# Attention by 128-token tile over all heads, transposes in bf16, woven by hand into an FFN of 512-token chunks

## The chip, the cores and the metric

One core of a Trainium2 chip runs the whole program; the other cores of the chip are idle. The metric is device time in microseconds (us): the median of repeated executions. TensorE is PE in the profile (PEld its weight loads), VectorE is DVE, ScalarE ACT, GpSimd POOL, and SyncE SP, which here only issues DMAs.

## The reference

Attention with a short window, then a maxout FFN. Each query sees the 8 first keys and the 96 last ones up to itself, with a bias that falls linearly with distance (ALiBi); softmax without anything unusual. The shapes are batch 4, 8 heads, 768 tokens, 64 columns a head; the FFN takes 3,072 rows of 512 through three weights of 512 x 768, keeps the largest of the three products, and multiplies by 768 x 512. All inputs and outputs are fp32.

```python
scores = scale * np.matmul(q, k.transpose(0, 1, 3, 2))
keep = is_global | is_local          # first 8 keys, or 0 <= distance < 96
scores = np.where(keep, scores + bias, -1e9)
a = softmax(scores)
x = np.matmul(a, v)                  # to rows of batch*seq, 8 heads x 64
h = np.maximum(np.maximum(x @ w1, x @ w2), x @ w3)
out = h @ w_out
```

## The kernel before, in words

The attention is tiled by batch and by pair of heads (lines 119 and 120): 16 pairs, each over all 768 tokens, that is six tiles of 128. Q, K and V of a pair come in by six DMAs (143 to 145) on two queues, SP for q and k, ACT for v. POOL casts v (149) and makes a second copy vg (150, 151) whose first 8 rows are the first 8 tokens, so that the block on the left of the diagonal can serve the global keys too. PE transposes twelve tiles of q and k in fp32 (161) into PSUM; ACT and DVE bring them to bf16 in SBUF as qT and kT (164 to 170). Scores (186, 196) are computed with keys on the partitions; ACT takes exp of them (203), and DVE multiplies by wmask, which holds the exponential of the bias and zero outside the window (209, 213). Then PE multiplies with v and a column of ones (235), DVE takes the reciprocal of the sums (242) and normalises (243), PE transposes the result in bf16 (249), and DVE writes it into xT (251), which holds all 3,072 tokens.

The FFN runs over six chunks of 512 tokens (256). For each of six blocks of 128 hidden columns PE computes three products of four matmuls each (263) into three PSUM banks, ACT copies the first out (269), DVE takes the maximum with the second and third (270, 271) into ht. Four output tiles of 128 tokens then take six matmuls each (275) into a PSUM tile, ACT copies it out (278), SP stores it (279). The weights come in while the third pair is set up (121 to 134).

Nothing in this text fixes the order of an engine's work: the code is written pair by pair and then chunk by chunk, and the framework's scheduler orders each engine's queue, so that FFN work of a batch whose four pairs are done mixes with the attention of the next batch. A chunk needs all heads of its tokens, so the first can begin when batch 0 is through, and the last batch has chunks of earlier tokens beside it as long as the scheduler has any left. PSUM has eight banks: three rotate in psA (tp, sp, xtp and po), two in psU, three in psH.

Of the kernel before, what the change touches and what calls it, by code (L numbers as in the profile page):

```python
# [19 lines left out]
def kernel(  # L21
# [13 lines left out]
    nc = tc.nc  # L35
# [6 lines left out]
    NHP = H // 2  # L42
    DM = H * D
    DFF = moe_w1.shape[1]
    NTOK = B * S
# [4 lines left out]
    for qc in range(1, NT):  # L50
        blocks.append((qc - 1, qc, True))
        blocks.append((qc, qc, False))
    NBLK = len(blocks)

    def dpos(qc):
        return 2 * qc

    def spos(qc):
        return 2 * qc - 1

    SGRP = [list(range(0, 4)), list(range(4, 8)), list(range(8, 11))]
    WKIND = [0 if (not b[2] and b[1] == 0) else (1 if not b[2] else 2)
             for b in blocks]

    persist = ctx.enter_context(tc.tile_pool(name="persist", bufs=1))
    wpool = ctx.enter_context(tc.tile_pool(name="wpool", bufs=1))
    qkv_pool = ctx.enter_context(tc.tile_pool(name="qkv", bufs=4))
    vv_pool = ctx.enter_context(tc.tile_pool(name="vv", bufs=3))
    qkT_pool = ctx.enter_context(tc.tile_pool(name="qkT", bufs=3))
# [26 lines left out]
    nc.vector.tensor_copy(rbase[:, 2, :], rbase[:, 2, :].bitcast(mybir.dt.int32))
    nc.gpsimd.affine_select(rbase[:, 2, :], rbase[:, 2, :], base=(NL - 1) - 128,
                            pattern=[[-1, 128]], channel_multiplier=1,
                            compare_op=ALU.is_ge, fill=BIGD)
    nc.vector.memset(rbase[0:NG, 2, :], float(NL))  # L100
    nc.vector.tensor_copy(rbase[:, 0, :], rbase[:, 1, :])
    nc.vector.tensor_scalar_min(rbase[0:NG, 0, :], rbase[0:NG, 0, :], float(NL))
    wmask = persist.tile([128, H, 3, 128], BF16, name="wmask")
    for h in range(H):
        nc.scalar.activation(wmask[:, h, :, :], rbase, AF.Exp,
                             bias=0.0, scale=-slopes[h])
# [11 lines left out]
    if True:  # L118
        for b in range(B):
            for jp in range(NHP):  # L120
# [196 lines left out]
```

## Time and profile before

| | |
|---|---|
| median of 3 runs | 285.93 us (285.15 to 286.02) |
| span of the profiled execution | 283.5 us |
| that execution's own time | not listed; the median is 2.4 us over its span |
| PE busy, matmuls | 237.2 us, 1,536 |
| DVE busy | 137.9 us |
| ACT busy | 102.4 us |
| POOL busy | 34.7 us |
| mean granted clock of PE | 0.916 |
| read from HBM, written | 25.17 MB, 6.29 MB |

A row of a view gives an engine, the line of the code, what it writes and reads, how often, and then busy time and mean. PEclk is the granted clock of TensorE: 1.00 is 2.4 GHz and 0.50 is 1.2 GHz. The chain of waits runs from the last instruction back to what released it, and is printed in order of time. Ends of matmuls are modelled, so a busy PE need not be at its peak.

### The profile page before, as it was taken

To read this page: it belongs to the slowest core of one execution; us is meant where nothing else is said; L and a number is where in the kernel's file an instruction comes from. 1 tells how busy PE (TensorE), PEld (TensorE's weight loads), DVE (VectorE), ACT (ScalarE), POOL (GpSimd) and SP (SyncE) were. 2 spreads that over 40 slices of the span, in tenths; PEclk is the share of its full clock that TensorE was granted. 3 is DMA by queue.
4 is the path that set the end of the run, shared out by engine and by line. 5 is a ranking of instruction groups with operands and counts; after the bars stand their busy time and mean duration, and the time that the engine had idled before them with its cause. 6 is when DMAs were issued, how large, how long until landed. Compare 5 with 4: busy or idle time off the path is not lost.

```text
span 283.5 us, 4068 instructions
## 1 busy us (share of the span) xinstructions
PE 237.2 (84%) x1536; PEld 126.2 (45%) x1536; DVE 137.9 (49%) x286; ACT 102.4 (36%) x198; POOL 34.7 (12%) x60
## 2 busy tenths in 40 slices
PE   0406668788999978999999788769999999999994
PEld 0303426446456446455455545534444444444441
DVE  1227654535759545658657554560251550551540
ACT  0435141452462452453554353242514214214222
POOL 2530202202112112012112200000000000000000
PEclk9999999775999995999999676676999999999999
DMA  8999999996373483370550000001513004003003
GB/s 167 218 333 355 310 269 225 216 186 147 79 168 74 97 168 84 85 166 5 111 112 2 0 2 0 0 2 54 205 39 141 7 0 150 0 0 149 2 0 149
DMA packets 81332, 31.73 MB, mean 112 GB/s; under 512 B 75936, under 2 KB 75936, under 8 KB 81312
## 3 DMA queue, kind: packets, MB, share of 16 engines
q1 hardware_dynamic: 56224, 25.17, 34.5%
q10 hardware_dynamic: 25088, 6.29, 11.5%
q8 instruction: 12, 0.20, 0.3%
q14 instruction: 8, 0.07, 0.1%
HBM read 25.17 MB, written 6.29 MB: 111 GB/s over the span
## 4 chain that ended last, share of the span: by engine, by line
PE 69%; DMA 12%; DVE 10%; ACT 6%; issue 2%; ACTq 0%; SPq 0%
PE h L263 33%; PE po L275 12%; PE tp L161 9%; DMA wst<-in_moe_w_dram 6%; PE sp L186 6%; ACT pt L203 5%; PE ut L235 4%; DVE pt L213 4%; DMA vraw<-in_v_dram 4%; PE xtp L249 3%; PE sp L196 3%; DVE xpair L243 3%; DMA wst<-in_moe_w_out_dram 2%; DVE rz L242 1%; DVE w L128 1%
## 5 line engine op out<-in xcount | busy, mean ns | idle before, releaser
L263 PE MATMUL h<-xT,w 128*128 128x512 bf16 x432 | 105.8, 387 | 0.4 <-ACT h L269 0.2
L263 PEld LDWEIGHTS <-w 128*128 128x128 bf16 x432 | 41.1, 99 | 43.6 <-issue 2.7
L203 ACT ACTIVATE pt<-sp 128x512 bf16<-128x512 f32 (+1 forms) x96 | 47.5, 564 | 30.5 <-PE sp L196 30.1
L270 DVE TENSOR_TENSOR h<-h,h 128x512 bf16<-128x512 bf16 x36 | 24.6, 682 | 40.6 <-PE h L263 39.8
L186 PE MATMUL sp<-qT,kT 64*128 64x256 bf16 x192 | 32.2, 294 | 13.1 <-DVE kT L168 12.2
L269 ACT CAST h<-h 128x512 bf16<-128x512 f32 x36 | 21.1, 585 | 53.6 <-PE h L263 46.7
L275 PE MATMUL po<-wo,ht 128*128 128x512 bf16 x144 | 34.1, 397 | 0.0
L235 PE MATMUL ut<-vql,pt 128*128 128x65 bf16 x224 | 22.9, 216 | 11.8 <-DVE pt L213 10.2
L271 DVE TENSOR_TENSOR ht<-h,h 128x512 bf16<-128x512 bf16 x36 | 24.6, 683 | 15.7 <-PE po L275 6.7
L213 DVE TENSOR_TENSOR pt<-pt,wmask 128x1280 bf16<-128x1280 bf16 x32 | 25.0, 821 | 13.1 <-ACT pt L203 13.1
L149 POOL CAST vql<-vraw 128x768 bf16<-128x768 f32 x16 | 13.2, 828 | 123.4 <-PE ut L235 115.5
L164 ACT ACTIVATE qT<-tp 128x512 bf16<-128x512 f32 x16 | 9.5, 596 | 49.3 <-PE tp L161 44.9
L235 PEld LDWEIGHTS <-pt 128*128 128x128 bf16 x352 | 18.0, 111 | 20.3 <-DVE pt L213 14.9
L161 PE MATMUL tp<-identf,qraw 128*128 128x128 f32 x96 | 19.2, 355 | 7.8 <-DMA qraw<-in_q_dram 7.8
L278 ACT COPY ost<-po 128x512 f32<-128x512 f32 x24 | 14.1, 587 | 30.9 <-PE po L275 30.8
L186 PEld LDWEIGHTS <-kT 64*128 64x128 bf16 x192 | 9.5, 97 | 31.4 <-DVE kT L168 21.2
L275 PEld LDWEIGHTS <-ht 128*128 128x128 bf16 x144 | 14.7, 102 | 18.3 <-issue 2.8
L196 PE MATMUL sp<-qT,kT 64*8 64x128 bf16 x128 | 19.7, 226 | 0.0
L161 PE MATMUL tp<-identf,kraw 128*128 128x128 f32 x96 | 19.5, 355 | 0.2
L249 PE MATMUL xtp<-identb,xpair 128*128 128x128 bf16 x96 | 10.9, 269 | 9.4 <-DVE xpair L243 8.8
L161 PEld LDWEIGHTS tp<-identf,qraw 128*128 128x128 f32 x96 | 15.1, 189 | 7.7 <-POOL vql L149 7.7
L243 DVE SCALAR_TENSOR_TENSOR xpair<-ut,rz 128x384 bf16<-128x384 f32 x32 | 17.7, 555 | 0.4
(35 smaller groups left out, 131.7 us busy)
## 6 DMA issues: line engine op xcount, KB each, us to landing
vraw<-in_v_dram ACTq DMA_DIRECT2D x32, 192.0 KB, 5.1
qraw<-in_q_dram SPq DMA_DIRECT2D x32, 192.0 KB, 3.8
kraw<-in_k_dram SPq DMA_DIRECT2D x32, 192.0 KB, 4.0
out_dram<-ost SPq DMA_DIRECT2D x24, 256.0 KB, 2.0
wst<-in_moe_w_dram SPq DMA_DIRECT2D x12, 384.0 KB, 6.3
wst<-in_moe_w_out_dram SPq DMA_DIRECT2D x6, 256.0 KB, 5.8
```

The lines of the kernel that those rows point to most:

```text
L161: nc.tensor.transpose(tp[:, i * 128:(i + 1) * 128], srcs[g * 4 + i], identf)
L186: nc.tensor.matmul(sps[hh][:, pos * 128:pos * 128 + w], kT[hsl, kt * 128:(kt + 1) * 128], qT[hsl, qc * 128:qc * 128 + w], start=True, stop ...
L196: nc.tensor.matmul(sps[hh][0:NG, pos * 128:(pos + 1) * 128], kT[hsl, 0:NG], qT[hsl, qc * 128:(qc + 1) * 128], start=True, stop=True)
L203: nc.scalar.activation(pts[hh][:, grp[0] * 128: grp[0] * 128 + n], sps[hh][:, 0:n], AF.Exp, bias=0.0, scale=1.0)
L213: eng.tensor_mul(pts[hh][:, 128:NBLK * 128].rearrange("p (a b c) -> p a b c", a=NT - 1, b=2), pts[hh][:, 128:NBLK * 128].rearrange("p (a b ...
L235: nc.tensor.matmul(ut[:, qc, :], pts[hh][:, bi * 128:(bi + 1) * 128], mov, start=(ci == 0), stop=(ci == len(cons) - 1), skip_group_check=True)
L243: nc.vector.scalar_tensor_tensor(out=xpair[:, :, hh, :], in0=ut[:, :, 0:64], scalar=1.0, in1=rz[:, :, None].to_broadcast([128, NT, 64]), o ...
L263: nc.tensor.matmul(ps[j], w123[dm][:, j, f * 128:(f + 1) * 128], xT[:, dm, c * CH:(c + 1) * CH], start=(dm == 0), stop=(dm == 3))
L269: nc.scalar.copy(h01, ps[0])
L270: nc.vector.tensor_max(h01, h01, ps[1])
L271: nc.vector.tensor_max(ht[:, f, :], h01, ps[2])
L275: nc.tensor.matmul(po, ht[:, f, tt * 128:(tt + 1) * 128], wo[:, f, :], start=(f == 0), stop=(f == 5))
```

## The change

The attention is no longer cut by pairs of heads but by tiles of 128 tokens, each with all eight heads, 24 tiles T in all. A tile is loaded by three DMAs, all on SP (function load). POOL casts q and k to bf16 in one instruction and v in another (cast). A tile's attention is split into units: X transposes q and k, eight 128x128 blocks in bf16, and DVE copies the result out in one instruction; POOL then makes kgT, a copy of the keys whose first 8 columns are the first 8 keys, so that window and global keys are one matmul for the left block, and vg likewise. S takes the scores of four heads into a PSUM tile of two banks, ACT takes exp of 1,024 columns at once (the scale now sits there), and DVE's mask multiply is put off until the next attention unit. A multiplies with v and normalises, for four heads. T transposes the result and writes it into xT of a 512-token chunk. FFN-1 units u_F1 have four matmuls, FFN-2 units u_F2 six.

The order of every engine's queue is now that of the program's text (manual_schedule). First come all units up to T of tile 3, the last tile of chunk 0; then each chunk's 22 FFN units are taken in turn, and after each of the first 20 one or two attention units of the next four tiles are written. The sixth chunk has none. The PSUM pools all have one buffer: S two banks, h0 to h2 one each, and one each for A, for X and T together (tag tp), and for the FFN output (po). Loads go out in a fixed list: tiles 0 to 3, w1 to w3 in nine DMAs, tile 4, w_out in three, then tiles 5 to 23 three ahead of use. The matmuls of the FFN are the same in number and shape.

```diff
--- the kernel before
+++ the kernel after
...
-    blocks = [(0, 0, False)]
...
-    xT = persist.tile([128, 4, NTOK], BF16, name="xT")
-
-    psA = ctx.enter_context(tc.tile_pool(name="psA", bufs=3, space=bass.MemoryType.PSUM))
-    psU = ctx.enter_context(tc.tile_pool(name="psU", bufs=2, space=bass.MemoryType.PSUM))
...
-        for b in range(B):
-            for jp in range(NHP):
...
-        for c in range(NCH):
...
+    CHUNK = 4
+    chunks = [list(range(c, c + CHUNK)) for c in range(0, NTT, CHUNK)]
...
+    raw_pool = ctx.enter_context(tc.tile_pool(name="raw", bufs=4))
+    cast_pool = ctx.enter_context(tc.tile_pool(name="cast", bufs=3))
+    qkT_pool = ctx.enter_context(tc.tile_pool(name="qkT", bufs=4))
+    kg_pool = ctx.enter_context(tc.tile_pool(name="kg", bufs=3))
+    p_pool = ctx.enter_context(tc.tile_pool(name="pp", bufs=5))
...
+    xb_pool = ctx.enter_context(tc.tile_pool(name="xb", bufs=3))
+    xT_pool = ctx.enter_context(tc.tile_pool(name="xT", bufs=3))
+    stage_pool = ctx.enter_context(tc.tile_pool(name="stage", bufs=12))
+    ht_pool = ctx.enter_context(tc.tile_pool(name="ht", bufs=2))
+    h01_pool = ctx.enter_context(tc.tile_pool(name="h01", bufs=3))
+    ost_pool = ctx.enter_context(tc.tile_pool(name="ost", bufs=4))
+    psS = ctx.enter_context(tc.tile_pool(name="psS", bufs=1, space=bass.MemoryType.PSUM))
+    psH = ctx.enter_context(tc.tile_pool(name="psH", bufs=1, space=bass.MemoryType.PSUM))
+    psO = ctx.enter_context(tc.tile_pool(name="psO", bufs=1, space=bass.MemoryType.PSUM))
+    psT = ctx.enter_context(tc.tile_pool(name="psT", bufs=1, space=bass.MemoryType.PSUM))
+    psP = ctx.enter_context(tc.tile_pool(name="psP", bufs=1, space=bass.MemoryType.PSUM))
...
+    def load(T):
+        b, t = divmod(T, NT)
+        r = raw_pool.tile([128, 3, H, D], FP32, name="raw", tag="raw")
+        raw[T] = r
+        sl = slice(t * 128, (t + 1) * 128)
+        for i, src in enumerate((q, k, v)):
+            nc.sync.dma_start(out=r[:, i], in_=src[b, :, sl, :].rearrange("h s d -> s h d"))
+
+    def cast(T):
+        b, t = divmod(T, NT)
+        r = raw[T]
+        qk = cast_pool.tile([128, 2, DM], BF16, name="qkb", tag="qkb")
+        qb[T] = qk
+        nc.gpsimd.tensor_copy(qk, r[:, 0:2].rearrange("p a h d -> p a (h d)"))
+        va[T] = va_first[b % 2] if t == 0 else va_ring[T % NVA]
+        nc.gpsimd.tensor_copy(va[T][:, :, 0:D], r[:, 2])
...
+    def make_vg(T):
+        b, t = divmod(T, NT)
+        if t == 0:
+            vg[T] = va[T]
+        elif t < NT - 1:
+            vg[T] = vg_ring[T % 3]
+            nc.gpsimd.tensor_copy(vg[T], va[T])
+            nc.gpsimd.tensor_copy(vg[T][0:NG], va[b * NT][0:NG])
+
+    def make_kg(T):
+        b, t = divmod(T, NT)
+        kT = qkT[T][:, 1]
+        if t == 0:
+            kgT[T] = kT
+            nc.gpsimd.tensor_copy(kg8[b % 2], kT[:, :, 0:NG])
+        elif t < NT - 1:
+            kgT[T] = kg_pool.tile([128, NP, 128], BF16, name="kgT", tag="kgT")
+            nc.gpsimd.tensor_copy(kgT[T], kT)
+            nc.gpsimd.tensor_copy(kgT[T][:, :, 0:NG], kg8[b % 2])
+
+    def u_X(T):
+        tp = psT.tile([128, 2, NP, 128], BF16, name="tp", tag="tp")
+        for a in range(2):
+            for jp in range(NP):
+                nc.tensor.transpose(tp[:, a, jp], qb[T][:, a, jp * 128:(jp + 1) * 128], identb)
+        qkT[T] = qkT_pool.tile([128, 2, NP, 128], BF16, name="qkT", tag="qkT")
+        nc.vector.tensor_copy(qkT[T], tp)
+        make_kg(T)
+        make_vg(T)
+        return []
+    def u_S(T, g):
+        b, t = divmod(T, NT)
+        sp = psS.tile([128, 2, 2, 2, 128], FP32, name="sp", tag="sp")
+        for ds in range(2 if t else 1):
+            for j2 in range(2):
+                jp = 2 * g + j2
+                for hh in range(2):
+                    hsl = slice(64 * hh, 64 * hh + 64)
+                    st = qkT[T][hsl, 1, jp] if ds == 0 else kgT[T - 1][hsl, jp]
+                    nc.tensor.matmul(sp[:, hh, j2, ds], st, qkT[T][hsl, 0, jp],
+                                     start=True, stop=True, skip_group_check=True)
+        P = p_pool.tile([128, 4, 2, 128], BF16, name="P", tag="P")
+        Pt[T, g] = P
+        spv = sp.rearrange("p a b d n -> p (a b) d n")
+        if t:
+            nc.scalar.activation(P, spv, AF.Exp, bias=0.0, scale=scale)
+            return [lambda: nc.vector.tensor_mul(P, P, wmask[:, g])]
+        nc.scalar.activation(P[:, :, 0], spv[:, :, 0], AF.Exp, bias=0.0, scale=scale)
+        return [lambda: nc.vector.tensor_mul(P[:, :, 0], P[:, :, 0], wmask0[:, g])]
...
+    def u_A(T, g):
+        b, t = divmod(T, NT)
+        op = psO.tile([128, 4, 65], FP32, name="op", tag="op")
+        P = Pt[T, g]
+        for j2 in range(2):
+            for hh in range(2):
+                h = 4 * g + 2 * j2 + hh
+                i = 2 * hh + j2
+                o = op[:, 2 * j2 + hh]
+                nc.tensor.matmul(o, P[:, i, 0], va[T][:, h], start=True, stop=(t == 0),
+                                 skip_group_check=True)
+                if t:
+                    nc.tensor.matmul(o, P[:, i, 1], vg[T - 1][:, h], start=False, stop=True,
+                                     skip_group_check=True)
+        if g == 0:
+            xb[T] = xb_pool.tile([128, H, D], BF16, name="xb", tag="xb")
+        x = xb[T]
+        rz = z_pool.tile([128, 4], FP32, name="rz", tag="rz")
+        nc.vector.reciprocal(rz, op[:, :, 64])
+        nc.vector.tensor_tensor(out=x[:, 4 * g:4 * g + 4], in0=op[:, :, 0:64],
+                                in1=rz[:, :, None].to_broadcast([128, 4, D]), op=ALU.mult)
+        return []
+
+    def u_XT(T):
+        c, i = divmod(T, CHUNK)
+        if i == 0:
+            xT[c] = xT_pool.tile([128, NP, CHUNK * 128], BF16, name="xT", tag="xT")
+        tp = psT.tile([128, NP, 128], BF16, name="xtp", tag="tp")
+        x = xb[T].rearrange("p h d -> p (h d)")
+        for jp in range(NP):
+            nc.tensor.transpose(tp[:, jp], x[:, jp * 128:(jp + 1) * 128], identb)
+        nc.vector.tensor_copy(xT[c][:, :, i * 128:(i + 1) * 128], tp)
+        return []
...
+    def u_F1(c, f, j):
+        if f == 0 and j == 0:
+            ht[c] = ht_pool.tile([128, NF, CHUNK * 128], BF16, name="ht", tag="ht")
+        ps = psH.tile([128, CHUNK * 128], FP32, name=f"h{j}", tag=f"h{j}")
+        for dm in range(4):
+            nc.tensor.matmul(ps, w123[f // 2][:, dm, j, (f % 2) * 128:(f % 2) * 128 + 128],
+                             xT[c][:, dm], start=(dm == 0), stop=(dm == 3))
+        if j == 0:
+            h01 = h01_pool.tile([128, CHUNK * 128], BF16, name="h01", tag="h01")
+            h01s[c, f] = h01
+            nc.scalar.copy(h01, ps)
+        elif j == 1:
+            nc.vector.tensor_max(h01s[c, f], h01s[c, f], ps)
+        else:
+            nc.vector.tensor_max(ht[c][:, f], h01s[c, f], ps)
+        return []
+
+    def u_F2(c, tt):
+        po = psP.tile([128, DM], FP32, name="po", tag="po")
+        for f in range(NF):
+            nc.tensor.matmul(po, ht[c][:, f, tt * 128:(tt + 1) * 128], wo[:, f],
+                             start=(f == 0), stop=(f == NF - 1))
+        ost = ost_pool.tile([128, DM], FP32, name="ost", tag="ost")
+        nc.scalar.copy(ost, po)
+        T = chunks[c][tt]
+        nc.sync.dma_start(out=out[T * 128:(T + 1) * 128, :], in_=ost)
+        return []
...
+    def cast_w(g):
+        nc.scalar.copy(w123[g][:, :, 0], wst[g, 0])
+        nc.vector.tensor_copy(w123[g][:, :, 1], wst[g, 1])
+        nc.gpsimd.tensor_copy(w123[g][:, :, 2], wst[g, 2])
+
+    def cast_wo(i):
+        nc.scalar.copy(wo[:, 2 * i:2 * i + 2], wst["o", i])
...
+    with tc.manual_schedule():
+        load(0)
...
+        loads = [lambda T=T: load(T) for T in range(1, 4)]
+        loads += [lambda g=g: load_w(g) for g in range(3)]
+        loads += [lambda: load(4), load_wo] + [lambda T=T: load(T) for T in range(5, NTT)]
...
+        att = []
+        att.append(("P", -1))
+        for i in range(NTT + 1):
+            if i < NTT:
+                att.append(("S", i, 0))
+            if i >= 1:
+                att.append(("A", i - 1, 1))
+            if i < NTT:
+                att.append(("S", i, 1))
+            if i + 1 < NTT:
+                att.append(("X", i + 1))
+            if i >= 1:
+                att.append(("T", i - 1))
+            if i < NTT:
+                att.append(("A", i, 0))
...
+        def emit_att(u):
+            tick()
+            if u[0] == "P":
+                upto(1)
+                cast(0)
+                upto(2)
+                cast(1)
+                u_X(0)
+                upto(3)
+            elif u[0] == "S":
+                for fn in u_S(u[1], u[2]):
+                    deferred.append((0, fn))
+            elif u[0] == "A":
+                u_A(u[1], u[2])
+            elif u[0] == "X":
+                T = u[1]
+                u_X(T)
+                if T + 1 < NTT:
+                    cast(T + 1)
+                upto(T + 3)
+            else:
+                u_XT(u[1])
...
+        att_until(("T", chunks[0][-1]))
+        cast_w(0)
+        for c in range(NCH):
+            ffn = [(u_F1, (c, f, j)) for f in range(NF) for j in range(3)]
+            ffn += [(u_F2, (c, tt)) for tt in range(CHUNK)]
+            if c + 1 < NCH:
+                stop = ("T", chunks[c + 1][-1])
+                end = att.index(stop) + 1
+            else:
+                end = len(att)
+            n = end - pos
+            slots = len(ffn) - 2
+            start = pos
+            for s, (fn, a) in enumerate(ffn):
+                fn(*a)
+                if c == 0 and fn == u_F1 and a[2] == 2:
+                    if a[1] in (0, 2):
+                        cast_w(a[1] // 2 + 1)
+                    if a[1] >= 3:
+                        cast_wo(a[1] - 3)
+                want = start + min(n, (n * (s + 1) + slots - 1) // slots)
+                while pos < want:
+                    emit_att(att[pos])
+                    pos += 1
+        tick()
...
```

Two places show the new order. On DVE, while attention and FFN are mixed: before (h and ht are the FFN's maxima of lines 270 and 271; pt<-pt,wmask the mask multiply; kT the copy of transposed keys; xT that of the transposed result):

```order
L209 TENSOR_TENSOR pt<-pt,wmask 128x128 x2
L213 TENSOR_TENSOR pt<-pt,wmask 128x1280 x2
L242 RECIPROCAL rz<-ut 128x6
L270 TENSOR_TENSOR h_2185<-h_2185,h_2171 128x512
L243 SCALAR_TENSOR_TENSOR xpair<-ut,rz 128x6x64
L242 RECIPROCAL rz<-ut 128x6
L148 MEMSET vql 128x12
L271 TENSOR_TENSOR ht<-h_2185,h_2172 128x512
L243 SCALAR_TENSOR_TENSOR xpair<-ut,rz 128x6x64
L251 COPY xT<-xtp 128x768
L270 TENSOR_TENSOR h_2204<-h_2204,h_2190 128x512
L170 CAST kT<-tp 128x512
```

and after, the piece from the second mask multiply of one tile to that of the next (P<-P,wmask is the mask multiply; qkT<-tp the copy behind X; xT<-xtp the copy behind T; xb<-op,rz the normalising):

```order
L153 TENSOR_TENSOR P<-P,wmask 128x1024
L132 COPY qkT<-tp 128x1024
L206 TENSOR_TENSOR h_1104<-h_1104,h_1130 128x512
L188 COPY xT<-xtp 128x4x128
L208 TENSOR_TENSOR ht<-h_1104,h_1143 128x512
L175 RECIPROCAL rz<-op 128x4
L176 TENSOR_TENSOR xb<-op,rz 128x256
L153 TENSOR_TENSOR P<-P,wmask 128x1024
L175 RECIPROCAL rz<-op 128x4
L176 TENSOR_TENSOR xb<-op,rz 128x256
L206 TENSOR_TENSOR h_1178<-h_1178,h_1193 128x512
L208 TENSOR_TENSOR ht<-h_1178,h_1210 128x512
```

A head pair's two wide multiplies and two normalisings over 768 tokens have become two multiplies and two normalisings for each 128 tokens, and the second multiply stands directly ahead of the copy of the next tile's transposes.

On SP, the queue of the loads, at the start of the program: before

```order
L143 DMA qraw<-in_q_dram 128x6x64
L144 DMA kraw<-in_k_dram 128x6x64
L126 DMA wst<-in_moe_w_dram 128x768 x12
L132 DMA wst_395<-in_moe_w_out_dram 128x512
...
L132 DMA wst_410<-in_moe_w_out_dram 128x512
```

and after

```order
L95 DMA raw<-in_k_dram 128x8x64
L95 DMA raw<-in_v_dram 128x8x64
L230 DMA wst<-in_moe_w_dram 128x4x256 x9
L95 DMA raw<-in_q_dram 128x8x64
L95 DMA raw<-in_k_dram 128x8x64
L95 DMA raw<-in_v_dram 128x8x64
L237 DMA wst<-in_moe_w_out_dram 128x2x512 x3
```

The weights stood behind the loads of four head pairs' q and k; now they stand behind those of tiles 0 to 3, and one tile stands between w1 to w3 and w_out.

## Rows read from the trace of the kernel before

**Rows 1.** The page: span, and busy time of each engine with its share

```profile
span 283.5 us, 4068 instructions
...
PE 237.2 (84%) x1536; PEld 126.2 (45%) x1536; DVE 137.9 (49%) x286; ACT 102.4 (36%) x198; POOL 34.7 (12%) x60
```

**Rows 2.** The page: the span in 40 slices of 7.09 us

```profile
PE   0406668788999978999999788769999999999994
...
PEclk9999999775999995999999676676999999999999
...
GB/s 167 218 333 355 310 269 225 216 186 147 79 168 74 97 168 84 85 166 5 111 112 2 0 2 0 0 2 54 205 39 141 7 0 150 0 0 149 2 0 149
```

**Rows 3.** Stretches of 1 us, PE alone: length, busy, PEclk, DMA share, GB/s

```profile
52.00:53.00 1.00, 0.01 (x1) 0.86 1.22 216
...
149.00:150.00 1.00, 0.82 (x13) 1.00 0.07 8
...
158.00:159.00 1.00, 0.29 (x6) 0.76 0.00 0
...
165.00:166.00 1.00, 0.88 (x8) 0.82 0.00 0
```

**Rows 4.** The chain of waits, in order of time: start us, us, what

```profile
49.45 0.15 PE sp L196 x2
...
122.30 1.32 PE tp L161 x12
...
125.12 0.32 PE sp L186 x4
...
129.80 0.30 PE ut L235 x10
...
132.56 0.34 PE xtp L249 x6
...
161.06 0.82 PE xtp L249 x6
...
238.36 15.54 PE h L263 x72
...
274.62 5.20 PE po L275 x24
279.88 0.59 ACT ost L278
```

**Rows 5.** Groups by shape: busy us, mean ns, idle before

```profile
L203 ACT ACTIVATE pt<-sp 128x512 bf16<-128x512 f32 x64 | 34.0, 599 | 26.4 <-PE sp L196 26.0
...
L213 DVE TENSOR_TENSOR pt<-pt,wmask 128x1280 bf16<-128x1280 bf16 x32 | 25.0, 821 | 13.1 <-ACT pt L203 13.1
...
L271 DVE TENSOR_TENSOR ht<-h,h 128x512 bf16<-128x512 bf16 x36 | 24.6, 683 | 15.7 <-PE po L275 6.7 <-PE h L263 6.6
...
L243 DVE SCALAR_TENSOR_TENSOR xpair<-ut,rz 128x384 bf16<-128x384 f32 x32 | 17.7, 555 | 0.4
...
L203 ACT ACTIVATE pt<-sp 128x384 bf16<-128x384 f32 x32 | 15.2, 495 | 4.1 <-PE sp L196 4.0
...
L149 POOL CAST vql<-vraw 128x768 bf16<-128x768 f32 x16 | 13.2, 828 | 123.4 <-PE ut L235 115.5 <-DMA vraw<-in_v_dram 7.9
...
L150 POOL COPY vg<-vql 128x520 bf16<-128x520 bf16 x16 | 9.9, 620 | 2.8 <-DVE vql L148 2.1
...
L251 DVE COPY xT<-xtp 128x768 bf16<-128x768 bf16 x16 | 8.9, 557 | 10.1 <-PE xtp L249 10.1
...
L209 DVE TENSOR_TENSOR pt<-pt,wmask 128x128 bf16<-128x128 bf16 x32 | 7.2, 225 | 16.0 <-ACT pt L203 16.0
```

**Rows 6.** Timeline of DVE and POOL, 25 to 30 us: start us, us, engine, line

```profile
25.03 0.56 DVE L128 CAST w<-wst 128x768 bf16<-128x768 f32 x1 [0.47 <-DMA wst<-in_moe_w_dram]
...
27.86 0.83 POOL L149 CAST vql<-vraw 128x768 bf16<-128x768 f32 x1 [11.33 <-PE ut L235]
28.00 1.10 DVE L128 CAST w<-wst 128x768 bf16<-128x768 f32 x1
```

More of the change, by code (lines that the diff above doesn't have):

```diff
@@ L41 @@
     NT = S // 128
-    NHP = H // 2
+    NTT = B * NT
+    NP = H // 2
     DM = H * D
     DFF = moe_w1.shape[1]
-    NTOK = B * S
+    NF = DFF // 128
     scale = 1.0 / math.sqrt(D)
     slopes = [2.0 ** (-8.0 * (h + 1) / H) for h in range(H)]
-    blocks = [(0, 0, False)]
[L50 to L59, printed above, removed]
@@ L61 @@
-    SGRP = [list(range(0, 4)), list(range(4, 8)), list(range(8, 11))]
-    WKIND = [0 if (not b[2] and b[1] == 0) else (1 if not b[2] else 2)
-             for b in blocks]
-    persist = ctx.enter_context(tc.tile_pool(name="persist", bufs=1))
[L66 to L69, printed above, removed]
@@ L104 @@
-    for h in range(H):
-        nc.scalar.activation(wmask[:, h, :, :], rbase, AF.Exp,
-                             bias=0.0, scale=-slopes[h])
-    w123 = [wpool.tile([128, 3, DFF], BF16, name=f"w123_{i}", tag=f"w123_{i}")
-            for i in range(4)]
-    wo = wpool.tile([128, 6, DM], BF16, name="wo")
-    wsrc = [moe_w1, moe_w2, moe_w3]
-    xT = persist.tile([128, 4, NTOK], BF16, name="xT")
-    psA = ctx.enter_context(tc.tile_pool(name="psA", bufs=3, space=bass.MemoryType.PSUM))
-    psU = ctx.enter_context(tc.tile_pool(name="psU", bufs=2, space=bass.MemoryType.PSUM))
@@ new lines @@
+    wmask = persist.tile([128, 2, 4, 2, 128], BF16, name="wmask")
+    wmask0 = persist.tile([128, 2, 4, 128], BF16, name="wmask0")
+    NVA = 4
+    va_ring = [persist.tile([128, H, 65], BF16, name=f"va{i}") for i in range(NVA)]
+    va_first = [persist.tile([128, H, 65], BF16, name=f"vaf{i}") for i in range(2)]
+    vg_ring = [persist.tile([128, H, 65], BF16, name=f"vg{i}") for i in range(3)]
+    kg8 = [persist.tile([128, NP, NG], BF16, name=f"kg8_{i}") for i in range(2)]
+    w123 = [persist.tile([128, 4, 3, 256], BF16, name=f"w123_{i}") for i in range(3)]
@@ new lines @@
+    wo = persist.tile([128, NF, DM], BF16, name="wo")
+    raw, qb, kb, qkT, kgT, Pt, ops, xb, rzs = {}, {}, {}, {}, {}, {}, {}, {}, {}
+    xT = {}
+    va, vg = {}, {}
+    def load(T):
[13 more added lines that the diff above has]
+        nc.gpsimd.tensor_copy(va[T][:, :, 0:D], r[:, 2])
@@ new lines, with load_w, load_wo @@
+    wst = {}
+    def load_w(g):
+        for j in range(3):
+            st = stage_pool.tile([128, 4, 256], FP32, name="wst", tag="wst")
+            wst[g, j] = st
+            nc.sync.dma_start(out=st, in_=wsrc[j][:, g * 256:(g + 1) * 256].rearrange(
+                "(i p) f -> p i f", p=128))
+    def load_wo():
+        for i in range(3):
+            st = stage_pool.tile([128, 2, DM], FP32, name="wst", tag="wst")
+            wst["o", i] = st
+            nc.sync.dma_start(out=st, in_=moe_w_out[i * 256:(i + 1) * 256, :].rearrange(
+                "(i p) f -> p i f", p=128))
```

252 lines of the change are left out of this document (64 added, 188 removed).

## The prediction

> **What bounds the kernel now.** Read the page's busy shares first [rows 1]: PE is busy 84% of 283.5 us, every other engine under half. But the page's slices [rows 2] show that this busy time is not all useful: PEclk is 5 to 7 tenths near 50 us, near 65 us and from 157 to 192 us, so PE looks busy while it runs at half speed. The one-microsecond stretches [rows 3] tell what went before: the clock is at 1.00 beside a PE busy share of 0.82 at 149 us; it drops in 52-53 us, where PE was busy for 0.01 us, and in 158-159 us, where it was busy for 0.29, and comes back in 165-166 us after several microseconds of nearly full work. Those lulls lie where a head pair's attention stands alone and PE, ACT and DVE wait for each other in turn. The chain of waits [rows 4] then gives the prices, since it shows the same work at both clocks: six bf16 transposes take 0.34 us at 132.56 and 0.82 us at 161.06. The last third of the kernel is FFN alone and PE-bound.
>
> The profiled span is 283.5 us and the median of the runs 285.93, so 2.4 us lie around the span; I work in span and add them at the end.
>
> **Prices at full clock** [rows 4]. FFN-1 unit of 4 matmuls: 15.54/72 x 4 = 0.86 us. FFN-2 unit of 6: 5.20/24 x 6 = 1.30. A bf16 transpose 0.34/6 = 0.057, where an fp32 one costs 1.32/12 = 0.110: the 192 of q and k save 10 us of PE work. An AV matmul 0.30/10 = 0.03. Scores of 64 x 128 columns do not exist before in this shape; below, half of a 256-column one, 0.32/4/2 = 0.040 us; above, the 128-column one of line 196, 0.15/2 = 0.075. I take 0.0625, nearer to the latter because each of them loads its own weights as that one does. So one token tile costs PE: X 8 x 0.057 = 0.45, T 0.23, two A 0.50, two S of eight 1.00, together 2.18 us.
>
> ACT and DVE prices are read from rows of two widths [rows 5]: exp from 384 and 512 columns (0.495, 0.599) gives 1.02 us for 1,024; mask multiply from 128 and 1,280 (0.225, 0.821) 0.69; the qkT copy, by line 251's 0.557 for 768 bf16 columns from PSUM, 0.69; xT copy of 512 0.42; normalise 128x256 by line 243's 0.555 for 384, 0.42; a reciprocal of 4 columns 0.2, just under line 209's 0.225 for 128. POOL: casting 1,024 columns 1.04 and 512 columns 0.61 by line 149, the 520-column copies 0.62.
>
> **Step 1, the start.** The first FFN matmul stands behind T(3) in PE's order, and that behind X(5), so behind tile 5's load; the third FFN unit stands behind a POOL cast of w that is queued behind the cast of tile 6. On SP all 6.29 MB of weights go ahead of tiles 5 and 6. Tiles 0 to 5 and the weights are 6 x 0.79 + 6.29 = 11.0 MB, tile 6 makes 11.8. By the page's GB/s line [rows 2], 7.09 us a slice, before moves 9.8 MB in five slices and 11.7 in six: 11.0 MB at 39.9 us and 11.8 at 42.9. w1 to w3 now arrive in 1 KB pieces instead of 3 KB, a price that lies between the 218 GB/s of the slice with q, k and v alone and the 355 of one with weights: 13 to 22 us for 4.7 MB. I take 2 us extra, so 41.9 and 44.9 us (bounds 40 and 50). Cast, transposes, T: first FFN unit at 44.1. POOL: 44.9 + 1.04 + 0.61 + 1.04 = 47.6 for the third unit, with 2.7 us of other PE work before it: a wait of 0.8. The attention of tiles 0 to 3 lies under the loads; without FFN units between, the chain of step 2 with S, X and T at half clock makes some 6 us a tile, and from the first exp near 10 us (behind the mask's own exponentials) four tiles are done by 34 us, before tile 5 has landed.
>
> **Step 2, the woven stretch.** A tile period holds five FFN units and six attention units: PE 5 x 0.86 + 2.18 = 6.50 us. DVE: 2 x 0.69 + 0.69 + 0.42 + 2 x 0.62 = 3.73 for attention, plus 3.33 maxes of 0.683 [rows 5], 6.0 in all; ACT 3.0; POOL 3.7. PE is the bound, but not alone: tp and xtp share one PSUM buffer, so T(i-1) waits until DVE has copied X(i+1) out, and DVE's order has the mask multiply of S(i,1) ahead of that copy. From the end of S(i,1): 0.2 to ACT (0.06 is the step from 279.82 to 279.88 [rows 4], the rest allows for the last matmul to drain), exp 1.02, multiply 0.69, copy 0.69, hops 0.1 = 2.70 us. PE has F 0.86, X 0.45, F 0.86 = 2.17 to do. It waits 0.53: period 7.0 us. The other single buffers have slack: sp is read out 1.2 us after S, the next S comes 2 us later; a bank of h has three slots.
>
> The fourth tile of a chunk has two FFN-2 units: 3 x 0.86 + 2.60 + 2.18 = 7.4; po has one buffer now where three rotated, so between two FFN-2 units PE waits for ACT's 0.59 [rows 4] and two hops, 0.85, less what stands between: 0.85 - 0.45 = 0.40. Two more FFN-2 units come bare: 0.62 + 1.30 and 0.85 + 1.30. A chunk is 3 x 7.0 + 7.8 + 4.1 = 32.9 us; five are 164.5, less 2.2 for three first tiles with half of S and A.
>
> **Step 3, the end.** The sixth chunk has no attention left: 15.54 + 4 x 1.30 + 3 x 0.85 = 23.3 us. Then the last ost copy and store as now: 283.5 - 279.88 = 3.6 [rows 4].
>
> **Sum.** 44.1 + 0.8 + 162.3 + 23.3 + 3.6, plus 2 us because the FFN starts at half clock (an estimate: in [rows 3] too the clock returns only after some microseconds of work, here taken as 4 at half speed) and 1 us for weight casts on DVE and ACT in chunk 0: 237.1 span, and 2.4 around it: **239.5 us**. What is removed, the bare attention at half clock after 157 us, has no row of its own in this sum: it is in the place that the woven tiles take.
>
> **A rule against the change.** Before shows what happens when a DVE copy and a POOL operation meet: the w cast takes 0.56 us alone, and 1.10 when it starts 0.14 us into a POOL cast, ending 0.41 us after it [rows 6]. POOL now works 3.7 us of each 7 beside a busier DVE, where before it had 34.7 us in all [rows 1], and no multiply of line 213 ran beside it. The Trainium skill, page "SBUF — State Buffer", section "Who interferes with whom", says that a DVE instruction with two SBUF inputs also shuts out a reading GpSimd instruction and is shut out by one, for its whole length; the trace agrees for the copy, and nothing in it shows two inputs. By that rule the mask multiply would wait as the cast did, and the sum would be that of the second rival; without it, the sum stands.
>
> **Rivals.** *PE never waits.* If the 0.53 us at T is hidden and scores cost 0.040, a tile period is 6.14: 15 plain tiles save 0.86, five others 0.36, the loads 2 us: 15 + 2 less, 223 us. For it: the woven part of before ran at a full PE [rows 2]; against it: there tp and po rotated through three buffers. Chance 0.20.
>
> *DVE and POOL shut each other out.* Each tile has two multiplies; the one before the qkT copy is on T's chain, the other eats DVE's slack of 1.0 us. A wait can last up to the 1.04 us of POOL's longest cast. At 0.6 to 1.0 us more a tile, 20 tiles cost 12 to 20 us: 251 to 260. Chance 0.20.
>
> *The clock falls at each chunk's end*, where three waits of 0.4 to 0.85 us stand close together. A fall as at 158 us lasts 7 us [rows 3] and loses 3.5: six cost 21, 260 us. Against it: 0.82 busy held the clock at 149 us. Chance 0.06.
>
> *Slower: the array runs much of the woven stretch at 1.2 GHz*, because every period has a wait. Woven work of 162 us takes 162/(1 - s/2) if a share s of the time is at half clock; the kernel is slower than 286 once that adds 47 us, at s above 0.45. Against it: the falls of before came where PE worked 0.01 and 0.29 us of a microsecond [rows 3]; here it would rest 0.53 us in 7. Chance 0.04.
>
> **Numbers.** The forecast case, 229 to 249 us, has 0.50. The range 218 to 262 takes in the first two rivals and most of the third, with the bounds of scores (4.5 us down, 2 up) and of the start (2 down, 8 up). About 0.3% is what a measurement of this kernel can tell from no change. Faster 0.95, same 0.01, slower 0.04, the last rival.
>
> **What would show it.** Right: FFN-1 begins at 42 to 50 us, with tile 5's load the last releaser; then PE waits for DVE at xtp, near 0.5 us a tile, with PEclk 9 throughout; PE waits for ACT at po, about four times a chunk; the last chunk takes 23 us. Wrong: a mask multiply of clearly over 0.69 us (second rival), PEclk of 5 inside the weave (third and fourth), PE waiting at sp or h, or an FFN that starts before 40 or after 52 us.

## The result, and the profile after

The median after is 241.91 us (241.84 to 242.35, four runs) against 285.54 (284.84 to 286.02) before: a ratio of 0.852, interval 0.846 to 0.857. The profiled execution took 241.87. The prediction was 239.5. The page's first lines answer to [rows 1] and [rows 2]; a slice is now 6.0 us.

```profile
span 240.1 us, 4041 instructions
...
PE 188.0 (78%) x1568; PEld 98.2 (41%) x1568; DVE 134.3 (56%) x278; ACT 90.6 (38%) x131; POOL 78.6 (33%) x131
...
PE   0556215598889898987998877999879889889972
...
PEclk9999999999999999999999999999999999999999
...
GB/s 158 218 249 349 347 245 278 224 219 218 126 4 46 247 198 180 35 0 184 227 161 134 0 26 238 228 210 3 0 87 90 0 3 0 63 113 3 0 86 90
```

PE is busy 49 us less and the span is 43 us shorter, so PE's idle time hardly changed (46.3 us before, 52.1 now). Part of what went is busy time at half speed: the 5s to 7s of [rows 2] in PEclk are gone. Summed over stretches of 1 us, PE was busy before for 39 us at a PEclk of 0.50, and the same work takes half of that at full speed, so this part is about 20 of the 49 us. About 10 more are the transposes of q and k, 192 x (0.110 - 0.057) by the prediction's prices. The rest is not taken apart here; the scores have fewer columns too, 352 matmuls of 128 where before had 160 of 256 and 160 of 128. From the ninth slice to the last but one PE stands at 7 to 9 tenths: it waits a little in almost every tile.

The start, in the timeline (start us, us, engine, line, what; in brackets the idle time before it and what ended it):

```profile
42.32 1.04 POOL L102 CAST qkb<-raw 128x1024 bf16<-128x1024 f32 x1 [3.00 <-DMA raw<-in_k_dram]
...
43.41 1.03 PE L130 MATMUL tp<-identb,qkb 128*128 128x128 bf16 x8 [2.92 <-POOL qkb L102]
...
44.49 0.69 DVE L132 COPY qkT<-tp 128x1024 bf16<-128x1024 bf16 x1 [2.21 <-PE tp L130]
45.23 0.59 PE L187 MATMUL xtp<-identb,xb 128*128 128x128 bf16 x4 [0.78 <-DVE qkT L132]
...
45.85 0.42 DVE L188 COPY xT<-xtp 128x512 bf16<-128x512 bf16 x1 [0.68 <-PE xtp L187]
...
46.33 1.86 PE L199 MATMUL h<-xT,w 128*128 128x512 bf16 x4 [0.52 <-DVE xT L188]
...
50.89 0.59 PE L199 MATMUL h<-xT,w 128*128 128x512 bf16 x2
```

Tile 5's q and k let POOL cast them at 42.32. From there a strict row of steps runs to the first FFN matmul at 46.33: cast, X(5), qkT copy, T(3), xT copy.

One tile period in the weave, from T to T, in the timeline of all engines:

```profile
120.67 0.38 PE L187 MATMUL xtp<-identb,xb 128*128 128x128 bf16 x4 [0.20 <-DVE qkT L132]
...
124.50 0.29 PE L146 MATMUL sp<-qkT 64*128 64x128 bf16 x4
...
124.83 1.04 PE L199 MATMUL h<-xT,w 128*128 128x512 bf16 x4
...
124.94 1.02 ACT L152 ACTIVATE P<-sp 128x1024 bf16<-128x1024 f32 x1 [0.86 <-PE sp L146]
...
125.90 0.69 DVE L208 TENSOR_TENSOR ht<-h,h 128x512 bf16<-128x512 bf16 x1 [0.36 <-PE h L199]
...
126.51 0.68 DVE L153 TENSOR_TENSOR P<-P,wmask 128x1024 bf16<-128x1024 bf16 x1
...
127.11 0.68 DVE L132 COPY qkT<-tp 128x1024 bf16<-128x1024 bf16 x1
...
127.85 0.38 PE L187 MATMUL xtp<-identb,xb 128*128 128x128 bf16 x4 [0.67 <-DVE qkT L132]
...
128.07 1.03 PE L199 MATMUL h<-xT,w 128*128 128x512 bf16 x4
```

T starts at 120.67 and again at 127.85, a period of 7.18 us; the next one is at 135.12. The second T waited 0.67 for the qkT copy, and the rows between show the whole chain: S(i,1) at 124.50, exp to 125.96, mask multiply to 127.19, copy to 127.79. The exp was done at 125.96, but DVE had taken up a max of the FFN at 125.90, so the multiply began at 126.51, half a microsecond late.

The waits of PE (us in total, times, longest):

```profile
PE tp L130 <- POOL qkb L102: 19.4, 5, 9.0
PE xtp L187 <- DVE qkT L132: 12.8, 18, 1.5
PE po L214 <- ACT ost L217: 9.5, 17, 1.0
```

Of the 18 waits for the qkT copy, four lie ahead of the first FFN matmul and make 4.4 us; the 14 in the weave make 8.4.

The chunks, each from its first FFN matmul to the next one's, within 0.2 us (length, then busy us and count of PE, PEld, DVE, ACT and POOL, PEclk, DMA share, GB/s):

```profile
82.00:114.60 32.60, 29.54 (x265) 15.31 (x264) 20.77 (x44) 12.83 (x18) 10.90 (x17) 1.00 0.58 131
114.60:148.50 33.90, 29.74 (x265) 15.32 (x264) 22.39 (x44) 13.72 (x18) 13.21 (x20) 1.00 0.58 125
...
212.60:236.30 23.70, 21.19 (x96) 9.19 (x94) 8.24 (x12) 5.85 (x10) 0.00 (x0) 1.00 0.12 46
```

And the end, in the chain of waits (start us, us, what), which answers to the last lines of [rows 4]:

```profile
212.59 15.54 PE h L199 x72
...
234.15 0.59 ACT ost L217
...
234.78 1.47 PE po L214 x6
...
236.32 0.58 ACT ost L217
```

The last chunk's 72 FFN-1 matmuls take the same 15.54 us as before; behind each group of six at po stand ACT's 0.58 and the hops, where before 24 po matmuls ran through in 5.20.

### The profile page after: what moved, and what is told of

It is laid out like the page before. It is cut to its first block, busy times and chain, and to the rows that moved or that the text cites. A ratio compares the mean times of both kernels' runs of the same rounds, so it can differ in the third digit from the quotient of the medians.

```text
span 240.1 us, 4041 instructions
## 1 busy us (share of the span) xinstructions
PE 188.0 (78%) x1568; PEld 98.2 (41%) x1568; DVE 134.3 (56%) x278; ACT 90.6 (38%) x131; POOL 78.6 (33%) x131
## 5 line engine op out<-in xcount | busy, mean ns | idle before, releaser
L152 ACT ACTIVATE P<-sp 128x1024 bf16<-128x1024 f32 x40 | 41.0, 1024 | 49.1 <-PE sp L146 49.1
L153 DVE TENSOR_TENSOR P<-P,wmask 128x1024 bf16<-128x1024 bf16 x40 | 31.1, 778 | 5.9 <-ACT P L152 5.8
L130 PE MATMUL tp<-identb,qkb 128*128 128x128 bf16 x192 | 17.2, 242 | 19.4 <-POOL qkb L102 19.4
L102 POOL CAST qkb<-raw 128x1024 bf16<-128x1024 f32 x24 | 24.8, 1033 | 17.9 <-DMA raw<-in_k_dram 17.9
L132 DVE COPY qkT<-tp 128x1024 bf16<-128x1024 bf16 x24 | 16.5, 686 | 16.0 <-PE tp L130 15.9
L130 PEld LDWEIGHTS <-qkb 128*128 128x128 bf16 x192 | 14.2, 109 | 24.4 <-POOL qkb L102 20.6
L176 DVE TENSOR_TENSOR xb<-op,rz 128x256 bf16<-128x256 f32 x48 | 20.4, 424 | 1.7
L187 PE MATMUL xtp<-identb,xb 128*128 128x128 bf16 x96 | 10.0, 232 | 12.8 <-DVE qkT L132 12.8
L166 PEld LDWEIGHTS <-P 128*128 128x128 bf16 x192 | 15.5, 105 | 9.5 <-DVE xb L176 5.0
L146 PE MATMUL sp<-qkT 64*128 64x128 bf16 x224 | 16.0, 238 | 3.7 <-ACT P L152 1.7
L166 PE MATMUL op<-va,P 128*128 128x65 bf16 x160 | 16.5, 203 | 0.7 <-DVE xb L176 0.7
```

The lines of the kernel that those rows point to most:

```text
L102: nc.gpsimd.tensor_copy(qk, r[:, 0:2].rearrange("p a h d -> p a (h d)"))
L130: nc.tensor.transpose(tp[:, a, jp], qb[T][:, a, jp * 128:(jp + 1) * 128], identb)
L152: nc.scalar.activation(P, spv, AF.Exp, bias=0.0, scale=scale)
L153: return [lambda: nc.vector.tensor_mul(P, P, wmask[:, g])]
L166: nc.tensor.matmul(o, P[:, i, 0], va[T][:, h], start=True, stop=(t == 0), skip_group_check=True)
L176: nc.vector.tensor_tensor(out=x[:, 4 * g:4 * g + 4], in0=op[:, :, 0:64], in1=rz[:, :, None].to_broadcast([128, 4, D]), op=ALU.mult)
```

## The experiments

All are edits of the kernel after; only the last one's diff is shown against the run ahead of it. The kernel before took 284.0 to 284.3 us in the same batches.

**The weave undone.** All attention first, then all FFN; transposes, widths, casts and buffers stay as after, only xT has six buffers in place of three.

```diff
-    xT_pool = ctx.enter_context(tc.tile_pool(name="xT", bufs=3))
+    xT_pool = ctx.enter_context(tc.tile_pool(name="xT", bufs=6))
...
-        att_until(("T", chunks[0][-1]))
+        att_until(("T", NTT - 1))
...
-                end = att.index(stop) + 1
+                end = max(pos, att.index(stop) + 1)
```

> The changed kernel with the weave undone: all 24 tiles' attention first, then the six FFN chunks; everything else is kept. Theory (the weave carries the gain): in the changed kernel's trace a bare tile takes 5.75 us at half clock and T of tile 3 ends near 45 us; 20 more tiles make 160 us, six bare chunks of 15.5 + 5.2 + 2.45 us another 139, the tail 4: span near 303, time near 305 us, PEclk at 5 in the rows from 45 to 160 us. Rival (the gain comes from bf16 transposes and wider instructions, and the weave adds little): below 255 us.

Measured: 303.63 us in one run, 62 more than after and 20 more than the kernel before in that batch. Two T of the bare stretch, in its timeline:

```profile
95.03 0.59 PE L187 MATMUL xtp<-identb,xb 128*128 128x128 bf16 x4 [1.33 <-DVE qkT L132]
...
100.76 0.59 PE L187 MATMUL xtp<-identb,xb 128*128 128x128 bf16 x4 [1.48 <-DVE qkT L132]
```

A bare tile takes 5.73 us, and its four transposes 0.59, where a woven tile's take 0.38 (above). PE's busy time is 215.6 us for the work that takes 188.0 after: 28 of the 62 us are more busy time for the same matmuls, since the attention's run at half speed here, and the other 34 are waiting. So bf16 transposes and wide instructions without a weave lose to the kernel before, and the order carries the gain. It does so in both ways at once: FFN units fill the attention's waits, and by filling them keep the array at 2.4 GHz. But the kernel before was woven too, by the scheduler. What the cheaper work alone would gain in its order, or the new order with the old instructions, no run shows.

**A rotating PSUM tile for po.** The pool of po's single bank goes, and po takes the FFN's three banks in turn.

```diff
-    psP = ctx.enter_context(tc.tile_pool(name="psP", bufs=1, space=bass.MemoryType.PSUM))
...
-        po = psP.tile([128, DM], FP32, name="po", tag="po")
+        po = psH.tile([128, DM], FP32, name="po", tag=f"h{(tt + 1) % 3}")
```

> The FFN output tile po takes the banks of h in turn (idle then) in place of one bank of its own, so three buffers rotate as before the change. Theory (PE's waits for ACT at po are on the path: 1.48 us in each woven chunk, 2.45 in the last, 9.9 in all): 9 us less, near 233 us, no wait of po for ost left. Rival (DVE or the qkT chain would end last anyway, the wait only moves): 238 to 242 us.

Measured: 229.55 us (229.21 to 230.15), ratio to before 0.812 (0.806 to 0.819), 12.4 less than after where 9 was expected. No wait of po for ACT is left in its trace, and T's stays at 12.5 us. The waits view had shown 9.5 for po. The rest fits time that it books as busy: a group of six whose successor waits shows 1.47 us (the chain above), while in a row without waits it takes 1.30 [rows 4], so 0.17 us of the last matmul's drain stands in front of each wait: 17 x 0.17 + 9.5 = 12.4.

**A second buffer for the transposes.** psT gets two buffers; the bank comes from po, which now shares the third FFN bank.

```diff
-    psT = ctx.enter_context(tc.tile_pool(name="psT", bufs=1, space=bass.MemoryType.PSUM))
-    psP = ctx.enter_context(tc.tile_pool(name="psP", bufs=1, space=bass.MemoryType.PSUM))
+    psT = ctx.enter_context(tc.tile_pool(name="psT", bufs=2, space=bass.MemoryType.PSUM))
...
-        po = psP.tile([128, DM], FP32, name="po", tag="po")
+        po = psH.tile([128, DM], FP32, name="po", tag="h2")
```

> X and T get two PSUM buffers, so T no longer waits for DVE's copy of X; po takes the bank of h2, still one buffer, to free the bank. Theory (T's wait, 12.8 us in the trace over 18 times, is on the path): 10 to 12 us less, 230 to 232 us; the tile period falls from 7.2 to some 6.5 us and xtp waits for nothing. Rival (DVE, 6.1 us of 7.2 busy and in order, is the real bound, so the wait reappears at the next S, where qkT is needed): 4 us less or nothing, 237 to 242 us.

Measured: 237.02 us (236.38 to 238.37), 0.840 (0.831 to 0.849): only 4.9 less than after. The expectation missed, and the waits view says why: T's wait is gone, and a new one has come.

```profile
PE po L213 <- ACT ost L216: 9.9, 18, 1.0
PE po L213 <- DVE ht L207: 8.2, 6, 1.7
```

The third FFN bank is free only after DVE's last max of the chunk, so the first of po's matmuls waits for it; in the kernel after, only the sixth matmul needed that max, and the wait was 1.4 us in all. The edit brought its own cost, so it doesn't price T's wait. The next run does.

**Both.** Two buffers for the transposes, and po in turn through the three FFN banks (the two edits above).

> Both edits at once: two buffers for X and T, and po rotating over the three banks of h. Theory (both waits are on the path and independent): 19 to 21 us less, 221 to 223 us, what the rival 'PE never waits' of the prediction gave. Rival (DVE becomes the bound at 6.1 us of work and some waiting for ACT a tile): 226 to 232 us.

Measured: 218.57 us (218.10 to 219.96), 0.774 (0.767 to 0.781). Against the run with the rotating po alone, T's wait is worth 229.55 - 218.57 = 11.0 us, and the time is below the 221 to 223 expected. The view's 12.5 there is not this price. Its four waits ahead of the first FFN matmul make 4.4 us, and most of that lies under the loads: between these two runs the first FFN matmul moves only from 46.76 to 45.80, while PE's wait for POOL's cast rises from 19.8 to 22.5 us. The 14 waits in the weave, 8.1 us, with a drain of 0.17 each make 10.5, close to the 10 that are left. The page's slices:

```profile
PE   0466404279999899999999999999999999999992
```

From 49 us on, in slices of 5.4 us, PE is at 9 tenths in all but one and the last.

**POOL reads beside the mask multiply.** Two copies per tile of 1,152 bf16 columns from SBUF to SBUF are added on POOL behind the cast; nothing uses their result.

```diff
+                for _ in range(2):
+                    nc.gpsimd.tensor_copy(ddst, dsrc)
```

> The changed kernel with two more POOL copies of 1,152 bf16 columns a tile, SBUF to SBUF, after the cast of the next tile (dead work). They keep POOL reading while the second mask multiply of a tile, the one ahead of the qkT copy, wants to start, some 1.6 us after POOL is done now. Theory (the lock of the second rival exists, and costs little here only because it meets the first multiply): that multiply waits some 0.4 us a tile, T waits as much longer, 6 to 10 us more, 248 to 252 us, with a mean of the mask multiply above 0.9 us. Rival (no lock between two-input multiplies and POOL): 241 to 243 us, multiply as before.

Measured: 249.06 us (248.40 to 249.16), 0.878 (0.873 to 0.883), 7.1 more than after. In its timeline:

```profile
128.78 2.35 POOL L353 COPY ddst<-dsrc 128x1152 bf16<-128x1152 bf16 x2
...
130.46 1.21 DVE L155 TENSOR_TENSOR P<-P,wmask 128x1024 bf16<-128x1024 bf16 x1
...
132.32 0.38 PE L189 MATMUL xtp<-identb,xb 128*128 128x128 bf16 x4 [1.19 <-DVE qkT L134]
```

The multiply on T's chain takes 1.21 us in place of 0.68, and T waits 1.19. Over the kernel the multiply's mean rises from 778 to 1,063 ns, PE's wait for the qkT copy from 12.8 to 18.0 us, and that of po for the FFN's last max from 1.4 to 4.0. In many tiles it is the first multiply that is late, by up to 1.3 us, and not the second.

**POOL writes beside it.** The same place, but two fills of 1,152 fp32 columns, which read nothing.

```diff
+                for _ in range(2):
+                    nc.gpsimd.memset(ddst, 0.0)
```

> The same place and about the same POOL time, but two memsets of 1,152 fp32 columns, which write SBUF and read nothing. Theory (the lock is on what POOL reads): no longer than the changed kernel, 241 to 243 us, mask multiply within 0.02 us of its 0.778. Rival (any POOL access locks, or POOL's longer queue delays kgT and vg): 246 us or more.

Measured: 241.12 us (240.67 to 242.14), 0.851 (0.846 to 0.857), the time of the kernel after.

```profile
125.53 2.16 POOL L351 MEMSET ddst<- 128x1152 f32 x2
...
127.22 0.68 DVE L154 TENSOR_TENSOR P<-P,wmask 128x1024 bf16<-128x1024 bf16 x1
...
192.03 4.40 POOL L351 MEMSET ddst<- 128x1152 f32 x4
...
192.71 0.68 DVE L154 TENSOR_TENSOR P<-P,wmask 128x1024 bf16<-128x1024 bf16 x1
```

The first multiply shown begins inside POOL's two fills and runs 0.47 us beside them, the second lies wholly inside four; both take 0.68. Over the kernel the multiply's mean is 786 ns, against 778 after. POOL's added time alone therefore costs nothing here. The Trainium skill, page "SBUF — State Buffer", section "Who interferes with whom", says that a DVE instruction with two SBUF inputs contends with a GpSimd instruction that reads SBUF and not with one that only writes it; the two runs agree on both halves.

**The loads in the order of need.** Tiles 4 to 6 go up between the weights, and the first weight's cast behind X(4).

```diff
-        loads += [lambda g=g: load_w(g) for g in range(3)]
-        loads += [lambda: load(4), load_wo] + [lambda T=T: load(T) for T in range(5, NTT)]
+        loads += [lambda: load_w(0), lambda: load(4), lambda: load(5), lambda: load_w(1),
+                  lambda: load(6), lambda: load_w(2), load_wo]
+        loads += [lambda T=T: load(T) for T in range(7, NTT)]
...
+                if u == ("X", 4):
+                    cast_w(0)
...
-        cast_w(0)
```

> The changed kernel with another order of loads: only the first third of w1 to w3 goes ahead of tiles 4 and 5, the second third ahead of tile 6, the rest and w_out after it; the first third is cast ahead of tile 6's cast. Theory (step 1: the FFN starts late because 6.29 MB of weights go ahead of tile 5): tile 5 lands near 28 us, the FFN starts when the bare attention of tiles 0 to 4 is through, near 34 us in place of 45, and the time falls by 9 to 11 us, to 231 to 233 us. Rival (the attention of tiles 0 to 3, or the weights themselves, set the start): under 3 us.

Measured: 232.92 us (232.39 to 234.44), 0.821 (0.816 to 0.827), 9.0 less than after; the first FFN matmul starts at 36.77, where 34 was expected. The stretches of 1 us (columns as above) show what is late next:

```profile
51.00:52.00 1.00, 0.00 (x0) 0.00 (x0) 1.00 (x2) 0.00 (x0) 0.95 (x1) 1.00 1.16 256
52.00:53.00 1.00, 0.84 (x10) 0.70 (x11) 0.49 (x2) 0.00 (x0) 0.95 (x3) 0.92 1.13 226
53.00:54.00 1.00, 1.00 (x4) 0.30 (x2) 0.58 (x1) 0.00 (x0) 1.00 (x2) 0.50 1.25 233
```

PE waits here for tile 7's load and cast at 50 and 51 us, and behind the lull PEclk falls to 0.92 and 0.50.

**All three.** Both PSUM edits with these loads.

> Two buffers for X and T, po rotating over the banks of h, and the new order of loads, in one. Theory (three independent terms): 218.6 less 9 to 11, 207 to 210 us. Rival (with loads spread into the woven stretch the DMAs or the weight casts hold up the first chunk): 212 to 217 us.

Measured: 213.24 us (212.49 to 214.58), 0.753 (0.749 to 0.757): the 207 to 210 expected was missed, and the rival's 212 to 217 came. The loads are worth 5.3 here against 9.0 alone: the faster weave reaches tile 7 sooner, and PE waits 3.6 us for it near 50 us.

**Tiles 7 and 8 brought forward too.**

```diff
-                  lambda: load(6), lambda: load_w(2), load_wo]
-        loads += [lambda T=T: load(T) for T in range(7, NTT)]
+                  lambda: load(6), lambda: load(7), lambda: load_w(2), lambda: load(8), load_wo]
+        loads += [lambda T=T: load(T) for T in range(9, NTT)]
```

The casts of the third weight and of w_out move to later FFN units to match.

> The kernel with both PSUM edits and the new loads, once more with another order of the later loads: tile 7 goes ahead of the last third of w1 to w3, tile 8 ahead of w_out, and the casts of that third and of w_out are issued later. Theory (the gain of the loads shrank from 9 to 5 us because tile 7 landed late: PE stood still for some 3.5 us around 50 us and the clock fell behind it): the stall goes, 3 to 5 us less than 213.2, 208 to 210 us, first FFN matmul still near 34.5 us. Rival (the bytes needed by then, 13 MB with w_out, are the bound whatever their order, so the stall moves to the weights or w_out): 212 to 214 us.

Measured: 208.28 us (207.55 to 209.17), 0.735 (0.731 to 0.739), the fastest of all. Its page:

```profile
PE 183.9 (89%) x1568; PEld 98.1 (47%) x1568; DVE 135.6 (65%) x278; ACT 90.3 (44%) x131; POOL 83.2 (40%) x131
...
PE   0356766999899999999999999999999999999992
```

From the eighth slice on, at 36 us, PE is at 9 tenths in all but one and the last. Of PE's 23.5 us of idle time, 17.3 lie ahead of the first FFN matmul at 34.80 and 3.8 in the tail.

## Why the prediction was right, step by step

The forecast case held: a gain from filled waits and a steady clock, less a small wait at T in most tiles and three at po in each chunk. Against the trace of after:

| term | predicted | measured |
|---|---|---|
| first FFN matmul | 44.1 | 46.33 |
| from there to the last chunk | 0.8 + 162.3 + 2 + 1 = 166.1 | 212.59 - 46.33 = 166.3 |
| last chunk | 23.3 | 236.25 - 212.59 = 23.7 |
| tail | 3.6 | 240.1 - 236.25 = 3.9 |
| around the span | 2.4 | 241.87 - 240.1 = 1.8 |

The 2.4 came from a median and the span of another execution; every run that lists its own span, of before too, has 1.7 to 1.9.

**The start** was 2.2 us short. Tile 5 could be cast at 42.32 where 41.9 was said, so the load model was good in its sum. That is in part luck: it holds 2 us for the smaller pieces of the weights, but the two slices that carry little else moved 349 and 347 GB/s, near the 355 of before, so no run shows that price. What failed is the step "Cast, transposes, T: first FFN unit at 44.1". These steps were given 2.2 us and took 4.01. The prediction left out the qkT copy, 0.69, which T(3) waits for because tp and xtp share one buffer, and the xT copy, 0.42; the buffer's wait was priced in the weave and forgotten here. The rest, 0.7 us, lies in X and T, 1.03 and 0.59 at half speed, and in the hops; how the 2.2 splits is not on record. The 2 us for half speed fit: the first unit took 1.86 us, those after 50.89 1.03. The wait of 0.8 for the third unit's weight did not appear, since PE came there only at 50.89.

**The weave** came out at 7.18 and 7.27 us where 7.0 was said, and the chunks behind the first at 32.6, 33.9, 32.5 and 31.6, where the mean predicted was 162.3/5 = 32.5. That the total agrees to 0.2 us is luck, since errors inside cancel. Scores cost 0.33 us for eight (124.50 to 124.83), 0.041 each and not 0.0625: the lower bound. PE's work in the period shown is 6.34 us, not 6.50. But T's wait with the drain in front of it is 0.84 there, not 0.53, because the prediction's chain had no FFN work of DVE in it. DVE's order has a max of the FFN ahead of the multiply. Where it starts just before the exp ends, it delays the multiply by half a microsecond. In the period that ends at 120.67 the max started half a microsecond before the exp ended, at 119.26, and T waited 0.20:

```profile
118.24 1.02 ACT L152 ACTIVATE P<-sp 128x1024 bf16<-128x1024 f32 x1 [1.24 <-PE sp L146]
...
118.74 0.68 DVE L208 TENSOR_TENSOR ht<-h,h 128x512 bf16<-128x512 bf16 x1
119.33 0.68 DVE L153 TENSOR_TENSOR P<-P,wmask 128x1024 bf16<-128x1024 bf16 x1
```

The prediction put T's wait into the 15 plain tiles of five chunks, 15 x 0.53 = 8.0 us. The 14 waits in the weave of after make 8.4 + 14 x 0.17 = 10.8, and the experiment gives 11.0, one of them at the start; this term was 2 to 3 us short. Against it stand scores that cost some 6 us less over the weave (an estimate: 296 x 0.0215). Their bounds were added up wrongly too: at the prediction's own prices, 16 scores in 17 woven tiles and 8 in the other three, they are 6.7 us down and 3.7 up, not 4.5 and 2.

**po**: the prediction's waits were 0.40, 0.62 and 0.85 in a chunk and 3 x 0.85 in the last, 11.9 in all; the edit that removes them gained 12.4. There are three in a full chunk, as in its sum; its list of signs says four.

**Durations** by the nearest rows held within a few hundredths: exp 1.02, multiply 0.69 (0.68 alone, but 0.778 in the mean, see the second rival), qkT copy 0.69, POOL's cast 1.04.

```profile
L152 ACT ACTIVATE P<-sp 128x1024 bf16<-128x1024 f32 x40 | 41.0, 1024 | 49.1 <-PE sp L146 49.1
...
L153 DVE TENSOR_TENSOR P<-P,wmask 128x1024 bf16<-128x1024 bf16 x40 | 31.1, 778 | 5.9 <-ACT P L152 5.8
...
L132 DVE COPY qkT<-tp 128x1024 bf16<-128x1024 bf16 x24 | 16.5, 686 | 16.0 <-PE tp L130 15.9
```

**The rivals.** *PE never waits* did not happen here, but its price did: with both waits removed the kernel takes 218.57, below the 223 given for it. *DVE and POOL shut each other out* is true of the hardware and nearly without price here. It hits the first multiply of a tile, which lies beside POOL's casts and eats DVE's slack; the one on T's chain took 0.68 or 0.69 at full width in every woven tile. The prediction's sign for this rival, a multiply clearly over 0.69, did show in the mean, but not its 251 to 260 us. Only once did a long multiply reach PE in the weave:

```profile
138.19 0.61 POOL L104 CAST va<-raw 128x512 bf16<-128x512 f32 x1
138.63 1.77 DVE L153 TENSOR_TENSOR P<-P,wmask 128x1024 bf16<-128x1024 bf16 x1
138.75 1.03 POOL L102 CAST qkb<-raw 128x1024 bf16<-128x1024 f32 x1
...
140.87 0.68 DVE L208 TENSOR_TENSOR ht<-h,h 128x512 bf16<-128x512 bf16 x1
...
141.60 0.39 PE L214 MATMUL po<-wo,ht 128*128 128x512 bf16 x1 [1.07 <-DVE ht L208]
```

The multiply lasts 1.77 us beside two casts in a row, the max behind it is late, and the last matmul of a po group waits 1.07 us for it: that is the chunk of 33.9. *The clock falls at each chunk's end*, and *slower*: neither happened; from 50.89 on the woven FFN units keep to 1.03 us, and the last chunk, behind three waits of 0.33, 0.49 and 0.72 us at po, starts at full speed, 15.54 us for its 72 matmuls. In [rows 2] the prediction passed over one more slow slice of before, the 5 that begins at 106 us; no term of it rests on that.

## What to carry to other kernels

A weave pays twice where one half of the work leaves TensorE idle often enough to lose its clock, so price it at both clocks and compare it with the same instructions unwoven. Then count PSUM buffers along each engine's order: a tile that was rotated and now has one buffer costs its whole round trip through the reader at every use, and banks of the other half of the work may be free at just that time. When a wait is removed at the start or in the middle, bring the next load forward as well, or it takes the wait's place.

## What the runs showed of the hardware

The lock between DVE and POOL follows what POOL reads. A multiply with two SBUF inputs took 1.21 us beside copies that read SBUF and 0.68 beside fills that only write. Beside two casts in a row it took 1.77: it began at 138.63 and ended 0.62 us after the second cast, so it waited for both.

The PEclk row can't be trusted ahead of the first fall that it records: in these traces it reads 1.00 until then, whatever the level. After shows 1.00 from the start, but four bf16 transposes took 0.59 us at 45.23 and 0.38 at 127.85, and the FFN units 1.86 and 1.03: those are the two levels, 1.2 and 2.4 GHz. The unwoven kernel shows 9 throughout, with 0.59 at 95.03. There the duration of one shape tells the level.

The waits view understates what a wait is worth by the drain ahead of it, 0.17 us a time here: 9.5 us shown at po and 12.4 gained, 8.1 shown at T in the weave of the run with the rotating po and about 10 gained. Its totals also hold waits that cost little, as T's 4.4 us ahead of the first FFN matmul, where removing them gained 1.0.
